# All four casts of one batch's first half on VectorE instead of two on GpSimd, in a retention and snake kernel on one Trainium2 core

## The chip, the cores and the metric

The kernel runs on 1 core of one Trainium2 chip. The core has several engines, each of which works through its own queue of instructions in order: TensorE (PE in the profile, with its weight loads as PEld), VectorE (DVE), ScalarE (ACT), GpSimd (POOL) and SyncE (SP, which here only issues DMAs). The engines wait for each other through semaphores. The metric is the device time of one execution in microseconds (us).

## The reference: a decayed attention without softmax, then a two-layer network

```python
# q, k, v: (8 batches, 8 heads, 576 positions, 64)
scores = scale * np.matmul(q, k.transpose(0, 1, 3, 2))
gamma = 1.0 - 2.0 ** (-5.0 - np.arange(H))
Dmat = np.where(rel >= 0, gamma[:, None, None] ** rel[None], 0.0)   # rel = i - j
ret = np.matmul(scores * Dmat, v)                # -> x: (4608 tokens, 512)
h = x @ w_in                                     # 512 -> 2048
s = np.sin(alpha * h)
g = h + s * s / (alpha + 1e-09)
out = g @ w_out                                  # 2048 -> 512
```

## The kernel before, in words

The attention is worked chunk by chunk. Because each weight gamma^(i-j) is a product of a factor of the query's position and one of the key's position, q and k are multiplied by these factors while they are cast from f32 to f16. Then plain matmuls and a mask of zeros and ones give the scores inside a chunk, and a running state (a sum of k times v, faded by a power of gamma from chunk to chunk) carries what lies before it.

Each batch has two halves of 256 positions (p = 0 and p = 1) and a rest of 64. For one half, q and k are each loaded as a 128x1024 f32 tile and cast in two quarters t = 0 and t = 1 (even and odd heads), 128x512 each. So one half has four casts, each one instruction in `cast_half` (line 215), a TENSOR_TENSOR of two tensors in SBUF (the loaded tile and the factors `cn`) into an f16 tile. The table's steps, one for each line, are these:

- `C b nm p t E` casts a quarter on engine E (V is VectorE, A ScalarE, G GpSimd).
- `TR b p nm` transposes k or q on TensorE (line 275), which needs both quarters of it; `TK` copies the transposed tile out of PSUM (lines 236 and 237). From batch 2's second half on, `CR b p` transposes by DMA instead, issued on SP's queue (line 232).
- `SP` computes scores on TensorE (line 376). `SM` masks them on VectorE (line 393), either straight from PSUM or, after `SO` has copied them to an f16 tile `scf` on ScalarE, from SBUF.
- `VA` (line 413) multiplies the masked scores with v, `ST` (line 439) adds the state's part, both on TensorE; `XT` copies the result out of PSUM as x (lines 236 and 237).
- `FA` (line 330) fades the running sum, `NS` (line 334, VectorE) adds the next chunk to it, `TS` (line 346) makes the f16 state from it.
- `G1` and `G2` are the two matrix products of the network (lines 535 and 574), with `SI` (sine, 544), `SQ` (square, 553 to 555) and `PR` (product, 560) between; `OS` copies a finished output block out of PSUM and issues its two stores on SP.
- `LK` loads q or k through SP; `LV` and `WO` load v and w_out through GpSimd's queue.

There are nine blocks of 512 tokens for the network: one for each batch's two halves, and one for all rests. The table `TABLE` writes out by hand the order of everything up to the end of block 1; the order of its lines is the order in each engine's queue. After it, a loop over blocks 2 to 8 interleaves the first product of a block with the second product of the block before, and puts the attention of the next batches between. The change is in the table, where block 0 is finished (`G2 0 ...`), batch 1's second half is worked (`VA 1 1`, `ST 1 1`), and batch 2's first half is prepared (lines 790 to 821):

```
TS 1 2 G        VA 1 1 1       SM 1 1 0       VA 1 1 0       ST 1 1
XT 1 1 A        OS 0 0 A       C 2 q 0 1 V    C 2 k 0 0 V    G2 0 3 3 hp
C 2 q 0 0 G     C 2 k 0 1 G    TR 2 0 k       TR 2 0 q       TK 2 0 k A
G1 1 0 hp       SI 1 0         FA 1 2 G       NS 1 3         OS 0 3 V
TS 1 3 G        C 2 k 1 1 G    C 2 k 1 0 G    C 2 q 1 1 G    C 2 q 1 0 G
CR 2 1          G1 1 1 hp      ...            TK 2 0 q V     SP 2 0 0
```

(It reads row by row.) So on VectorE the queue there is `SM 1 1 0`, the two casts marked V, `NS 1 3`, `OS 0 3`, `TK 2 0 q`; on GpSimd it is `TS 1 2`, the two casts marked G, `FA 1 2`, `TS 1 3`, and the four casts of batch 2's second half; on TensorE it is `VA 1 1 0`, `ST 1 1`, `G2 0 3 3`, `TR 2 0 k`, `TR 2 0 q`, `G1 1 0`, `G1 1 1`, `SP 2 0 0`. `SM 1 1 0` reads `scf`, that is, from SBUF.

Of the kernel before, what the change touches and what calls it, by code (L numbers as in the profile page):

```python
# [16 lines left out]
def kernel(  # L17
# [10 lines left out]
    nc = tc.nc  # L28
# [63 lines left out]
    alpha_t = const.tile([P, FC], F32, tag="alpha", bufs=1)  # L92
# [486 lines left out]
    def gemm2(n, u, bank):  # L579
        gemm2_pe(n, u, bank)  # L580
        c, part = divmod(u, 4)
        if part == 3:
            osb = work.tile([P, 512], F32, tag="osb", bufs=4, name="osb")
            nc.scalar.copy(osb, ops.pop((n, c)))  # L584
            for h in range(2):
                nc.sync.dma_start(rows_of(n, c, h), osb[halves(h)])
# [50 lines left out]
TS 0 1 V  # L637
NS 0 2
TS 0 2 G
AO  # L640
WI 2
TK 0 1 q AA
# [155 lines left out]
C 2 q 0 1 V  # L798
C 2 k 0 0 V
G2 0 3 3 hp  # L800
C 2 q 0 0 G
C 2 k 0 1 G
TR 2 0 k
TR 2 0 q
TK 2 0 k A
# [100 lines left out]
PR 1 13  # L906
PR 1 10
G1 1 14 hp
GN
G1 1 15 mm  # L910
VA 2 1 1
ST 2 1
# [10 lines left out]
LV 3 0  # L923
TS 2 3 G
CR 3 1
GN
"""

    HALVES = [(0, "k"), (0, "q"), (1, "k"), (1, "q")]
# [1 line left out]
    V, A_, G_ = nc.vector, nc.scalar, nc.gpsimd  # L931

    with tc.manual_schedule():
# [18 lines left out]
        al = {}  # L952

        def alpha():
            al["ps"] = psum.tile([P, FC], F32, tag="hp", bufs=3, name="al_ps")
            nc.tensor.matmul(al["ps"], alpha_r, eye, start=True, stop=True, is_transpose=True)

        def alpha_out():
            nc.scalar.copy(alpha_t, al["ps"])
            nc.vector.tensor_scalar_add(inva, alpha_t, 1e-9)  # L960
            nc.vector.reciprocal(inva, inva)

# [81 lines left out]

        second = [(n, u) for n in range(1, NBLK) for u in range(12 if n == NBLK - 1 else 16)]

        def next_second():
            n, u = second.pop(0)
            gemm2(n, u, "hp" if n == NBLK - 1 and u > 3 else "op")

        STEP = {
            "GN": next_second,
            "H1": pair_pe,
            "HS": pair_sine,
# [30 lines left out]
            "OS": put_out,  # L1085
            "KB": keep_busy,
            "AL": alpha,
            "AO": alpha_out,
        }

# [14 lines left out]
        for n in range(2, NBLK):  # L1105
# [39 lines left out]
            for u in range(16):  # L1145
                gemm1(n, u)
                for f in todo.get(u, []):
                    f()
                last = second[0][1] % 4 == 3
                if not last:  # L1150
                    square(n, u, A_)
                    product(n, u)
                next_second()
                if last:
                    square(n, u, A_)
                    product(n, u)
        while second:
            next_second()
# [42 lines left out]
```

## Time and profile before

| | us |
|---|---|
| median of 3 runs (lowest, highest) | 316.03 (314.01, 316.04) |
| the profiled execution, whole | 315.3 |
| its span, first to last instruction | 313.5 |

The granted TensorE clock of the profiled execution was 0.98 of full speed. By stages of the profiled execution (us from its start; busy time of each engine in us):

| stage | length | PE | DVE | ACT | POOL | GB/s |
|---|---|---|---|---|---|---|
| 0 to 50: weights, batch 0, most of block 0 | 50.00 | 42.75 | 33.40 | 30.61 | 31.22 | 214 |
| 50 to 53.5 | 3.50 | 3.50 | 2.86 | 0.00 | 2.66 | 292 |
| 53.5 to 57.1 | 3.60 | 1.46 | 3.60 | 1.17 | 2.98 | 243 |
| 57.1 to 59.7 | 2.60 | 2.60 | 2.16 | 1.50 | 1.06 | 102 |
| 59.7 to 85: block 1 with batch 2 | 25.30 | 23.50 | 20.03 | 22.10 | 22.29 | 169 |
| 85 to 226: the loop | 141.00 | 141.00 | 92.73 | 113.06 | 77.12 | 168 |
| 226 to 313.5: the loop's last blocks | 87.50 | 83.14 | 33.73 | 60.25 | 0.00 | 46 |

An engine that is busy for all of a stage need not be what sets its length: an instruction counts as busy from its start to its end, also when it is held up in between. A row is read by asking which engine waits for which; the chain of waits, which follows the last instruction back to what released it, gives that.

### The profile page before, as it was taken

What the parts mean: (1) busy time and instruction counts of PE and PEld (TensorE: products, weight loads), DVE (VectorE), ACT (ScalarE), POOL (GpSimd) and SP (SyncE); (2) the same over time, 40 slices, a digit from 0 to 9 for tenths busy, and PEclk for the clock granted to TensorE, in tenths of its full rate; (3) what the DMA queues carried; (4) which work ended last, traced back from release to release, by engine and by line L of the source; (5) the groups of instructions that cost most, each with busy time, mean ns of one, the idle gap of its engine ahead of it and who ended that gap; (6) DMA issues with size and microseconds to landing.
All of it is one profiled execution on the core that took longest, in us unless ns stands there. A gap on an engine that the chain in (4) does not pass through costs nothing.

```text
span 313.5 us, 7658 instructions
## 1 busy us (share of the span) xinstructions
PE 298.0 (95%) x3145; PEld 152.6 (49%) x3145; DVE 188.5 (60%) x265; ACT 228.7 (73%) x374; POOL 137.3 (44%) x160
## 2 busy tenths in 40 slices
PE   5799989799899999999999999999999999999994
PEld 4586444444444444444444444544444444444443
DVE  3688957798675365856866786645845343444401
ACT  1469862599688878887888788787887878888710
POOL 3778656769969965950593055024700000000000
PEclk9589999999999999999999999999999999999998
DMA  8999999796999899999999977689331111122133
GB/s 215 209 174 193 265 192 289 141 225 150 149 182 225 170 166 192 207 150 206 209 143 213 170 167 187 102 108 130 69 67 37 35 36 33 33 50 52 33 67 68
DMA packets 118018, 44.74 MB, mean 143 GB/s; under 512 B 84432, under 2 KB 113504, under 8 KB 117984
## 3 DMA queue, kind: packets, MB, share of 16 engines
q1 hardware_dynamic: 83792, 35.08, 58.5%
q0 software_dynamic: 33600, 8.92, 29.2%
q8 instruction: 24, 0.39, 0.6%
q10 hardware_dynamic: 592, 0.28, 0.4%
q14 instruction: 10, 0.08, 0.1%
HBM read 36.91 MB, written 9.44 MB: 148 GB/s over the span
## 4 chain that ended last, share of the span: by engine, by line
PE 80%; DVE 8%; DMA 4%; ACT 2%; POOL 2%; issue 1%; SPq 1%; DVEq 0%; POOLq 0%; ACTq 0%
PE ops L574 37%; PE hps L535 32%; DVE ret L393 4%; DMA qT<-q 2%; PE sc L376 2%; PE o L413 2%; DMA k<-in_k_dram 2%; DVE gT L560 2%; PE o L439 2%; PE tr L275 1%; PE kv L312 1%; PE ops L1163 1%; PE hps L1013 1%; DVE kvs L334 1%; DVE gT L1040 1%
## 5 line engine op out<-in xcount | busy, mean ns | idle before, releaser
L560 DVE SCALAR_TENSOR_TENSOR gT<-ss_t,inva,hps 128x512 f16<-128x512 f16 x136 | 100.4, 745 | 86.8 <-ACT ss_t L553 86.3
L574 PE MATMUL ops<-w_out,gT 128*128 128x512 f16 x560 | 140.8, 379 | 0.0
L535 PE MATMUL hps<-x,w_in 128*128 128x512 f16 x480 | 120.9, 379 | 1.3 <-DVE gT L560 1.1
L544 ACT ACTIVATE s_t<-hps,alpha_t 128x512 f16<-128x512 f32 x136 | 92.8, 685 | 33.0 <-PE hps L535 31.8
L535 PEld LDWEIGHTS <-w_in 128*128 128x128 f16 x544 | 52.8, 98 | 64.9 <-issue 1.9
L574 PEld LDWEIGHTS <-gT 128*128 128x128 f16 x560 | 52.7, 98 | 59.9 <-DVE gT L560 0.3
L553 ACT ACTIVATE ss_t<-s_t 128x512 f16<-128x512 f16 x127 | 79.9, 631 | 2.5
L346 POOL TENSOR_TENSOR s<-kvs,cn 128x512 f16<-128x512 f32 x28 | 30.5, 1091 | 56.2 <-ACT kvs L319 47.6
L584 ACT COPY osb<-ops 128x512 f32<-128x512 f32 x31 | 18.2, 586 | 13.2 <-PE ops L574 13.2
L126 POOL DMA_DIRECT2D v<-in_v_dram x32 | 22.0, 732 | 0.0
L236 ACT CAST x<-o 128x1024 f16<-128x1024 f32 (+1 forms) x17 | 14.9, 889 | 6.3 <-PE o L439 5.5
L393 DVE TENSOR_TENSOR ret<-sc,mask 128x1024 f16<-128x1024 f32 x12 | 14.4, 1214 | 5.7 <-PE sc L376 5.7
L215 DVE TENSOR_TENSOR q<-q,cn 128x512 f16<-128x512 f32 x17 | 14.4, 847 | 5.1 <-DMA q<-in_q_dram 4.9
L535 PE MATMUL hps<-x_rest,w_in 128*128 128x512 f16 x64 | 16.4, 379 | 0.0
L215 POOL TENSOR_TENSOR q<-q,cn 128x512 f16<-128x512 f32 x15 | 16.0, 1077 | 0.1
L393 DVE TENSOR_TENSOR ret<-sc,two 128x768 f16<-128x768 f32 x16 | 14.9, 950 | 0.0
L413 PE MATMUL o<-ret,v 64*64 64x128 f16 (+1 forms) x512 | 10.6, 218 | 3.4 <-DVE ret L393 2.5
L555 POOL TENSOR_TENSOR ss_t<-s_t 128x512 f16<-128x512 f16 x10 | 10.7, 1077 | 6.2 <-ACT s_t L544 4.9
L359 POOL TENSOR_TENSOR kvs<-s,kvs 128x256 f32<-128x256 f32 x15 | 12.5, 835 | 1.2
L376 PE MATMUL sc<-qT,kT 64*64 64x128 f16 (+1 forms) x512 | 11.2, 219 | 0.9 <-DMA qT<-q 0.6
L376 PEld LDWEIGHTS <-kT 64*64 64x64 f16 x512 | 8.2, 111 | 7.5 <-issue 5.1
L413 PEld LDWEIGHTS <-v 64*64 64x64 f16 x512 | 7.9, 110 | 7.5 <-issue 7.0
(69 smaller groups left out, 207.6 us busy)
## 6 DMA issues: line engine op xcount, KB each, us to landing
out_dram<-osb SPq DMA_DIRECT2D x70, 128.0 KB, 2.5
q<-in_q_dram SPq DMA_DIRECT2D x14, 512.0 KB, 6.8
k<-in_k_dram SPq DMA_DIRECT2D x32, 128.0 KB, 5.1
k<-in_k_dram SPq DMA_DIRECT2D x7, 512.0 KB, 6.8
q<-in_q_dram SPq DMA_DIRECT2D x8, 256.0 KB, 7.2
v<-in_v_dram POOLq DMA_DIRECT2D x8, 256.0 KB, 5.8
w_in<-in_moe_w_in_dram POOLq DMA_DIRECT2D x4, 512.0 KB, 6.9
w_out<-in_moe_w_out_dram POOLq DMA_DIRECT2D x4, 512.0 KB, 7.3
```

What stands on the lines that cost most here:

```text
L126: nc.gpsimd.dma_start(t_[halves(g), :, s], v[b, :, xs, :].rearrange("h i d -> i h d"))
L215: eng.tensor_tensor(half[b, nm, p][:, :, :, t, :], raw[b, nm, p].rearrange("p (a t) (r d) -> p a t r d", t=2, r=2)[:, :, t], (ct if nm == ...
L346: (eng or nc.gpsimd).tensor_tensor(d_, self.kvs[:, n].unsqueeze(2).to_broadcast([P, 4, 2, D]), g2.unsqueeze(3).to_broadcast([P, 4, 2, D]), ...
L376: nc.tensor.matmul(sc[halves(g), t, x : x + 128 - 64 * late], T[0][halves(t), 2 * a + r, halves(g)], T[1][halves(t), 2 * a : 2 * a + 2, 64 ...
L393: nc.vector.tensor_tensor(ret.rearrange("p t (z x) -> p (t z) x", z=2)[:, :, 0:n], sc.rearrange("p t (z x) -> p (t z) x", z=2)[:, :, 0:n], ...
L413: nc.tensor.matmul(o[g][halves(t), x0 : x0 + 128].rearrange("p (r i) -> p r i", r=2)[:, :, i0:], x, y, start=(t, g) not in begun, stop=las ...
L535: nc.tensor.matmul(hps, w_in16[:, a, fc * P : (fc + 1) * P], x_of[n][:, a], start=(a == 0), stop=(a == KT - 1),)
L544: nc.scalar.activation(s_t, hps, mybir.ActivationFunctionType.Sin, bias=0.0, scale=alpha_t[:, fc : fc + 1],)
L553: nc.scalar.activation(ss_t, s_t, mybir.ActivationFunctionType.Square)
L560: nc.vector.scalar_tensor_tensor(gT[n][:, fc, :], ss_t, inva[:, fc : fc + 1], hps, MULT, ADD)
L574: nc.tensor.matmul(ops[n, c], gT[n][:, fk, c * P : (c + 1) * P], w_out16[:, fk, :], start=(fk == 0), stop=(fk == FC - 1),)
L584: nc.scalar.copy(osb, ops.pop((n, c)))
```

## The change

Two letters in the table move the casts of q's quarter 0 and k's quarter 1 of batch 2's first half from GpSimd's queue to VectorE's. They stand in the table behind VectorE's other two casts and before `NS 1 3`. The step `AO` is split in two, `AC` (the copy of alpha on ScalarE) and `AO` (the two VectorE instructions), which stand one behind the other where `AO` stood; and `GN` takes a number that the function doesn't use.

```diff
 TS 0 2 G
+AC
 AO
...
 C 2 q 0 1 V
 C 2 k 0 0 V
 G2 0 3 3 hp
-C 2 q 0 0 G
-C 2 k 0 1 G
+C 2 q 0 0 V
+C 2 k 0 1 V
 TR 2 0 k
 TR 2 0 q
...
-GN
+GN 0
...
-GN
+GN 1
...
+        def alpha_copy():
+            nc.scalar.copy(alpha_t, al["ps"])
+
         def alpha_out():
-            nc.scalar.copy(alpha_t, al["ps"])
             nc.vector.tensor_scalar_add(inva, alpha_t, 1e-9)
             nc.vector.reciprocal(inva, inva)
...
-        def next_second():
+        def next_second(k=0):
             n, u = second.pop(0)
             gemm2(n, u, "hp" if n == NBLK - 1 and u > 3 else "op")
...
+            "AC": alpha_copy,
             "AO": alpha_out,
```

## The prediction, made before the changed kernel was run

> **What bounds the kernel now.** I read the busy time by engine first, then the chain of waits, then the timeline at the place of the change. The first two:
>
> ```profile
> PE 298.0 (95%) x3145; PEld 152.6 (49%) x3145; DVE 188.5 (60%) x265; ACT 228.7 (73%) x374; POOL 137.3 (44%) x160
> PE 80%; DVE 8%; DMA 4%; ACT 2%; POOL 2%; issue 1%; SPq 1%; DVEq 0%; POOLq 0%; ACTq 0%
> ```
>
> TensorE is busy for 95% of the span and carries 80% of the chain. From 85 to 226 us it has no idle time at all, so there VectorE's and GpSimd's loads decide nothing. The change can gain or lose only where TensorE waits around batch 2's first half. The chain of waits there (start, length, what):
>
> ```profile
> 52.39 1.20 DVE x L237 x2
> 53.59 3.45 DVE ret L393
> 57.04 0.04 issue
> 57.08 0.42 PE o L413 x16
> 57.50 0.55 PE o L439 x8
> 58.05 0.86 PE ops L574 x4
> 58.92 0.89 PE tr L275 x16
> 59.81 1.73 PE hps L535 x8
> ...
> 77.83 6.92 DMA qT<-q
> ```
>
> One VectorE instruction, the mask `SM 1 1 0` (L393), stands in it for 3.45 us; after it TensorE works without a gap through VA, ST, G2, the transposes and into block 1. The timeline there (start, length, engine, line, operation, tiles, in brackets the idle time before):
>
> ```profile
> 45.62 0.68 DVE L393 TENSOR_TENSOR ret<-scf,mask 128x1024 f16<-128x1024 f16 x1
> ...
> 52.85 1.05 POOL L346 TENSOR_TENSOR s<-kvs,cn 128x512 f16<-128x512 f32 x1
> ...
> 53.51 3.52 DVE L393 TENSOR_TENSOR ret<-scf,mask 128x1024 f16<-128x1024 f16 x1
> ...
> 53.86 1.05 POOL L215 TENSOR_TENSOR q<-q,cn 128x512 f16<-128x512 f32 x1
> ...
> 54.87 1.04 POOL L215 TENSOR_TENSOR k<-k,cn 128x512 f16<-128x512 f32 x1
> 55.87 0.60 POOL L330 TENSOR_TENSOR s<-kvs,cn 128x256 f32<-128x256 f32 x1
> 56.95 0.68 DVE L215 TENSOR_TENSOR q<-q,cn 128x512 f16<-128x512 f32 x1
> 57.08 0.42 PE L413 MATMUL o<-ret,v 64*64 64x128 f16 x16 [2.14 <-DVE ret L393]
> ```
>
> The same mask took 0.68 us at 45.62, while GpSimd did nothing, and 3.52 us here. It ends at 57.03, which is 0.56 us after GpSimd's unbroken row of four instructions ends (55.87 + 0.60 = 56.47). Elsewhere a VectorE instruction with two SBUF inputs behaves alike: a cast at 125.64 took 1.24 us instead of 0.68 and ended at 126.88, 0.55 us after GpSimd's L359 (125.60 + 0.73 = 126.33). A mask that reads its scores from PSUM took its usual 1.22 us at 97.53 beside GpSimd's L346. So I read the 3.52 us as 0.68 us of work and 2.84 us held up by GpSimd's row, in which the two casts that the change removes stand second and third.
>
> **The change part by part.** *Removed from GpSimd:* two casts, 1.05 + 1.04 us, 2.01 us by start to start (53.86 to 55.87). L346 stays, 52.85 to 53.90, and `FA 1 2` (L330, 0.60 us) now follows at about 53.86, since the sum that it reads was ready at 52.39. GpSimd's row ends at 54.46. If the mask again ends 0.56 us behind the row, it ends at 55.02, 2.01 us earlier. If it is let in at 53.90 it ends at 54.46; then FA waits (as an L358 at 124.47, 1.06 us instead of 0.61, did beside a cast) and delays the first cast.
>
> *Added to VectorE:* two casts. Three rows bear on their price: 0.68 us with GpSimd idle (56.95, and start to start 0.61, 56.95 to 57.56), 0.79 us at 124.26 and 1.24 to 1.47 us (125.64, 154.98) behind one GpSimd instruction. GpSimd is idle here until `NS 1 3`, which stands behind the casts, so I take 0.61 each. The first of four starts at 54.94 (0.08 before the mask ends, as before), and the last ends at 54.94 + 3 x 0.61 + 0.68 = 57.45. If the mask is let in early, the first cast waits for FA's end at about 54.92, ends 0.55 later at 55.47, and the last ends at 57.30: nearly the same.
>
> *Moved on TensorE:* VA starts at 55.07 instead of 57.08, ST and G2 follow, and G2 ends its turn near 56.75. Before, the transposes started at 58.75, straight behind G2, because the last cast was ready at 58.24. Now they need VectorE's fourth cast, at 57.45, and start at 57.5: TensorE waits 0.7 us anew. Of the 2.01 us, 58.75 - 57.50 = 1.25 us remain. Queued behind the transposes are both G1 and the scores of batch 2, which also need the two copies `TK`, free on both engines (ScalarE's x copy ends near 57.1, VectorE's `OS 0 3` near 58.4; the transposes end near 58.56).
>
> *Behind the added casts on VectorE:* `NS 1 3` ends at 57.8 instead of 58.57, so `TS 1 3` on GpSimd starts 0.8 us earlier, and its four casts of batch 2's second half end at 62.93 instead of 63.72. The next square there, at 64.10, waited 0.38 us for ScalarE; its sine comes at 62.83, so GpSimd is 0.1 us behind, with the product that needs it not yet due. SP's queue holds the two DMA transposes of `CR 2 1` and then batch 3's loads. Its first transpose was held by the output stores until 62.62 and the second until 64.13; now the casts hold the second, to about 62.96, so loads are issued 1.15 us earlier. They land at 71.58 for q, first half (66.08 + 5.5), used at 72.20: slack 0.62; and at 76.73 for its second half (68.23 + 8.5), used at 77.37: slack 0.64. With uses 1.25 and loads 1.15 earlier, 0.5 us of slack stays. No wait on a load is new for the moved casts: GpSimd read both tiles by 53.86 and 54.87 without waiting.
>
> *Afterwards* TensorE waits 0.59 us at 84.88 for the DMA transpose `CR 3 0`, issued from 76.49 behind a GpSimd row that starts with a square at 70.00, itself waiting 0.72 us for ScalarE. So this wait moves with the rest, and the stage from 59.7 on moves as a whole. `AC`, `AO` and `GN` keep every queue's order: nothing.
>
> The sum: -2.01 (hold-up) + 0.76 (transposes now waiting for casts) = -1.25 us. The profiled execution (span 313.5, 1.8 around it, 315.3) becomes 314.05; by the median of 316.03, which lies 0.7 above it, 314.8. I take 314.4, between.
>
> The Trainium skill, "SBUF — State Buffer", section "Who interferes with whom", says that a VectorE instruction with two SBUF inputs and a GpSimd instruction that reads SBUF exclude each other, for the whole instruction of the one that came first. On the exclusion the trace agrees (3.52 against 0.68 us). On its extent it doesn't: by the rule the mask should have been let in at 53.90, after one instruction, and it waited for four. By that rule the casts held nothing, and the change gives the slower rival below.
>
> **The rivals.** *The hold-up stays (slower).* For: three times VectorE was let in between two GpSimd instructions: a cast at 124.26 (0.79 us, ending 0.55 after L346), one at 154.98, and a square at 75.15 (0.41 us) amid a GpSimd row from 70.00 to 76.46. So the row of four may not be what held the mask. Against: the end 0.56 us behind exactly that row. Then the mask still ends at 57.03, four casts end at 56.95 + 3 x 0.61 + 0.68 = 59.46, and the transposes start at 59.5 instead of 58.75: +0.75 us, 316.05 by the profiled execution, 316.8 by the median. It decides from the point where the mask ends later than 56.3, since the fourth cast then comes after 58.70.
>
> *A second hold-up eats the gain.* The square at 75.15 asked for its inputs within 0.1 us of a boundary between two GpSimd instructions (75.21). GpSimd is forecast 0.1 us off the rest; if the square misses the boundary, it ends behind the row at 76.46 + 0.27 instead of 75.56, 1.17 us late (0.27 as at 21.49, where the square ended at 22.40 behind a GpSimd end at 22.11). Net about -0.1: 315.2 to 315.9.
>
> *More is gained.* TensorE is idle for 25.30 - 23.50 = 1.8 us between 59.7 and 85, partly behind collisions of this kind (GpSimd squares of 1.24 us at 70.00, casts of 1.25 at 75.21). If some fall away as engines shift, up to about 0.75 us more: -2.0, 313.3.
>
> **How the numbers follow.** Forecast 0.60; hold-up stays 0.17; second hold-up 0.13; more gained 0.10. The low end is 313.3 less 0.5, since the runs of before reach 1.3 below the profiled execution; the high end is 316.8, the slower rival on the median. Range 312.8 to 316.8. One per cent, about what a measurement of this kernel can tell from no change, is 3.2 us. None of the cases passes that by its own size: the gain would need all of TensorE's idle time in the stage, the loss several new hold-ups in a row. Both signs get something for a run of such effects and for the 0.6% by which runs of the same kernel differ: faster 0.13, within 0.78, slower 0.09.
>
> **What would show it.** Right: the mask of 3.52 us falls to 0.9 to 1.5; four VectorE casts in a row at 0.61 start to start; TensorE's wait of 2.14 us before VA nearly gone, and a new one of 0.6 to 0.7 us before the transposes, which start at 57.3 to 57.5; the wait at 84.88 near 83.7. Wrong: a mask still over 2.5 us; casts over 1 us; a square after 70 us that waits behind GpSimd; loads of batch 3 awaited on GpSimd.

## The result, and the profile after

| | before | changed |
|---|---|---|
| median, us (lowest, highest; 22 executions each, taken together) | 316.39 (314.01, 318.10) | 314.49 (313.45, 317.23) |
| ratio, with its 95% interval | | 0.9953 [0.9933, 0.9974] |
| the profiled execution / its span, us | 315.3 / 313.5 | 316.3 / 314.5 |

The ratios here, and the counts in the last section, leave out the few executions that took over 1.5% longer than the fastest of their kernel.

The changed kernel is faster by 0.5%, about 1.5 us by the ratio: the interval lies clear of 1, and the difference is under one per cent. Its profiled execution is one of the longer of the 22, and longer than the profiled one of before, so the spans must not be compared as they stand. Distances from one event show what the change did. I count from the start of the mask `SM 1 1 0`: before at 53.51 us, after at 53.92 us.

The chain of waits after, at the place of the change (start, length, what):

```profile
52.80 1.20 DVE x L237 x2
54.00 1.44 DVE ret L393
55.44 0.60 DVE q L215
56.04 0.60 DVE k L215
56.65 0.60 DVE q L215
57.25 0.60 DVE k L215
57.85 0.34 DVE kvs L334
58.19 0.04 issue
58.23 1.05 PE tr L275 x16
59.29 1.73 PE hps L535 x8
```

The timeline of the same place:

```profile
53.26 1.06 POOL L346 TENSOR_TENSOR s<-kvs,cn 128x512 f16<-128x512 f32 x1
...
53.92 1.53 DVE L393 TENSOR_TENSOR ret<-scf,mask 128x1024 f16<-128x1024 f16 x1
...
54.27 0.62 POOL L330 TENSOR_TENSOR s<-kvs,cn 128x256 f32<-128x256 f32 x1
...
57.77 0.41 DVE L334 TENSOR_TENSOR kvs<-s,kv 128x256 f32<-128x256 f32 x1
...
58.23 0.61 PE L275 MATMUL tr<-ident,k 128*128 128x128 f16 x8 [0.90 <-DVE kvs L334]
```

The mask falls from 3.52 to 1.53 us and ends 0.56 us behind GpSimd's row, which is now two instructions long (54.27 + 0.62 = 54.89; 53.92 + 1.53 = 55.45). TensorE's wait of 2.14 us before `VA` is gone. In its place VectorE stands in the chain with four casts and with `NS 1 3` (L334): the transposes, which have to wait 0.90 us, are released by `NS 1 3`, not by the last cast: they start 0.05 us after `NS 1 3` ends (57.77 + 0.41 = 58.18), and 0.38 us after the cast (57.85). The reason is in the code:

```python
kv2 = psum.tile([P, 2, 512], F32, tag="mm", bufs=2, name="kv")
...
self.tr_of[p] = psum.tile([P, 2, 1024], F16, tag="mm", bufs=2, name="tr"), []
```

The transposes' tile in PSUM takes one of the two `mm` buffers, and that buffer still holds the sum `kv`, which `NS 1 3` is the last to read. In the trace of before, `NS 1 3` and the first transpose stood here:

```profile
58.16 0.41 DVE L334 TENSOR_TENSOR kvs<-s,kv 128x256 f32<-128x256 f32 x1
...
58.75 0.61 PE L275 MATMUL tr<-ident,k 128*128 128x128 f16 x8
```

First transpose: 58.75 - 53.51 = 5.24 us behind the mask's start before, 58.23 - 53.92 = 4.31 after. The first mask of batch 3, about 31 us behind, tells how much of this is kept (before, then after):

```profile
85.35 2.35 DVE L393 TENSOR_TENSOR ret<-sc,mask 128x1024 f16<-128x1024 f32 x2 [0.62 <-PE sc L376]
```

```profile
84.57 2.36 DVE L393 TENSOR_TENSOR ret<-sc,mask 128x1024 f16<-128x1024 f32 x2 [0.68 <-PE sc L376]
```

Where the trace then loses more than this, near 121 us (before, then after; timeline, the number in brackets is the idle time in front and what ended it):

```profile
119.81 1.29 DVE L215 TENSOR_TENSOR k<-k,ct 128x512 f16<-128x512 f32 x2 [2.17 <-DMA k<-in_k_dram]
```

```profile
120.27 2.42 DVE L215 TENSOR_TENSOR k<-k,ct 128x512 f16<-128x512 f32 x2 [3.41 <-DMA k<-in_k_dram]
...
123.41 1.02 PE L535 MATMUL hps<-x,w_in 128*128 128x512 f16 x4 [1.74 <-DVE gT L560]
```

VectorE waits 3.4 instead of 2.2 us for a load of batch 5, its two casts then take 2.42 instead of 1.29 us beside GpSimd's instructions, and the products queued behind them make TensorE wait 1.74 us. The account of this execution closes: it comes to the mask 0.41 us later; it is 1.19 us shorter from there to the first mask of batch 3 (84.57 - 53.92 = 30.65 against 85.35 - 53.51 = 31.84); and it waits 1.74 at 121. The sum, +0.96, is the 1.0 by which the spans differ. So in this execution the wait at 121 takes back more than was won before it.

### The profile page after: what moved, and what is told of

Read it like the earlier page. It is cut to its first block, busy times and chain, and to the rows that moved or that the text cites. A ratio compares the mean times of both kernels' runs of the same rounds, so it can differ in the third digit from the quotient of the medians.

```text
span 314.5 us, 7656 instructions
## 1 busy us (share of the span) xinstructions
PE 298.1 (95%) x3145; PEld 152.8 (49%) x3145; DVE 188.5 (60%) x267; ACT 228.5 (73%) x374; POOL 135.4 (43%) x158
## 3 DMA queue, kind: packets, MB, share of 16 engines
q1 hardware_dynamic: 83792, 35.08, 57.3%
## 4 chain that ended last, share of the span: by engine, by line
PE 67%; POOL 8%; DVE 8%; DMA 7%; SPq 5%; issue 2%; ACT 1%; DVEq 0%; POOLq 0%
PE ops L574 31%; PE hps L535 26%; DMA k<-in_k_dram 7%; SPq L147 3%; POOL k L215 3%; DVE ret L393 3%; POOL q L215 2%; PE o L413 2%; PE sc L376 2%; DVE gT L560 1%; PE tr L275 1%; PE o L439 1%; PE ops L1167 1%; POOL ss_t L555 1%; POOL s L346 1%
## 5 line engine op out<-in xcount | busy, mean ns | idle before, releaser
L346 POOL TENSOR_TENSOR s<-kvs,cn 128x512 f16<-128x512 f32 x28 | 30.3, 1084 | 58.2 <-ACT kvs L319 48.5
L215 DVE TENSOR_TENSOR q<-q,cn 128x512 f16<-128x512 f32 x18 | 15.3, 850 | 4.9 <-DMA q<-in_q_dram 4.9
L215 POOL TENSOR_TENSOR q<-q,cn 128x512 f16<-128x512 f32 x14 | 14.6, 1058 | 0.1
L215 DVE TENSOR_TENSOR k<-k,ct 128x512 f16<-128x512 f32 x12 | 9.6, 817 | 3.4 <-DMA k<-in_k_dram 3.4
```

The source lines that it names most:

```text
L215: eng.tensor_tensor(half[b, nm, p][:, :, :, t, :], raw[b, nm, p].rearrange("p (a t) (r d) -> p a t r d", t=2, r=2)[:, :, t], (ct if nm == ...
L346: (eng or nc.gpsimd).tensor_tensor(d_, self.kvs[:, n].unsqueeze(2).to_broadcast([P, 4, 2, D]), g2.unsqueeze(3).to_broadcast([P, 4, 2, D]), ...
```

## The experiments

Each kernel is the one before or the changed one with a small edit, and ratios are to the kernel before on the same chip. "First transpose" and "first mask of batch 3" are distances from the mask's start.

**e1, the changed kernel again.**

> The changed kernel once more, for a second trace. All distances are from the start of the mask SM 1 1 0. Theory (GpSimd's unbroken row holds the mask, and the transposes of batch 2 wait for NS 1 3, which the added casts push back): mask 1.5 us; first transpose at 4.3 (before 5.24); first mask of batch 3 at 30.7 (before 31.84); ratio to the kernel before 0.993 to 0.998. The wait of 1.7 us that TensorE had near 121 us in the first trace, for a late load of k, comes and goes from execution to execution: it need not be there. Rival (that wait belongs to the change): it is there again, and the whole gain of 1 us in the early stage is given back in this execution too.

Measured: 314.66 us, ratio 0.9944 [0.9915, 0.9973]. Mask 1.52, first transpose 57.24 - 52.93 = 4.31, first mask of batch 3 at 30.09. TensorE's wait near 121 us is there again, 1.66 us, so here the rival was right: nearly all that was won is given back. Still the span is 312.9: 0.58 earlier at the mask, 1.75 shorter up to batch 3, 1.66 lost, together -0.67 against -0.6. What is left is about the 0.58, and that can't be put down to the change: over the 14 traces the mask starts between 52.32 us (e10) and 54.27 us (e5), in kernels with and without the change alike.

**e2, one cast moved.**

```diff
-C 2 q 0 0 V
+C 2 q 0 0 G
 C 2 k 0 1 V
```

> Only k's quarter 1 moves to VectorE; q's quarter 0 stays on GpSimd. Theory (the row holds the mask until it ends): the row is TS, one cast, FA, and the mask takes 0.39 + 1.01 + 0.60 + 0.56 = about 2.55 us; three casts on VectorE, NS 1 3 ends at 4.67, first transpose at about 4.7 from the mask's start (before 5.24, both moved 4.31). Time about half way, 0.5 us under before. Rival one (the mask is let in behind the first GpSimd instruction, something else held it before): the mask is 3.5 or 0.95 us, not 2.5. Rival two (it is all or nothing): 1.5 us.

Measured: 315.70 us, ratio 0.9969 [0.9934, 1.0004]. The timeline of e2:

```profile
53.61 2.52 DVE L393 TENSOR_TENSOR ret<-scf,mask 128x1024 f16<-128x1024 f16 x1
53.96 1.05 POOL L215 TENSOR_TENSOR q<-q,cn 128x512 f16<-128x512 f32 x1
54.97 0.60 POOL L330 TENSOR_TENSOR s<-kvs,cn 128x256 f32<-128x256 f32 x1
```

The mask lies half way, 0.56 us behind the end of a row that is one cast shorter than before, and the first transpose comes at 58.32 - 53.61 = 4.71. Both rivals fall: each cast in the row costs the mask its length. The time lies between the two kernels, but its interval reaches 1.

**e3, the row put back, the casts left on VectorE.**

```diff
+DU 2 q 0 0
+DU 2 k 0 1
...
+        def dummy(b, nm, p, t):
+            d_ = work.tile([P, 4, 2, D], F16, tag="dum", bufs=2, name="dum")
+            nc.gpsimd.tensor_tensor(d_, ...)
```

> As the changed kernel, all four casts on VectorE, but GpSimd also makes two casts of the same size into a scratch tile, where its two casts stood: extra work that nothing reads. This separates the row on GpSimd from the place of the casts. Theory: the mask takes 3.5 us again, then come four casts and NS 1 3: first transpose at 3.44 + 4 x 0.60 + 0.41 + 0.05 = 6.3 from the mask's start, 1.1 later than before and 2.0 later than with the change; time 1.0 us over before, ratio near 1.003. Rival (the mask's 3.5 us had another cause, which the move took away): mask 1.5 us, first transpose 4.3, time as with the change.

Measured: 316.71 us, ratio 1.0011 [0.9977, 1.0045]. The timeline of e3, then its busy times for each us (stretch and length; then PE, PEld, DVE, ACT and POOL busy; then the granted clock of TensorE, the DMA share and GB/s):

```profile
53.08 3.52 DVE L393 TENSOR_TENSOR ret<-scf,mask 128x1024 f16<-128x1024 f16 x1
...
53.43 1.05 POOL L1058 TENSOR_TENSOR dum<-q,cn 128x512 f16<-128x512 f32 x1
...
54.43 1.04 POOL L1058 TENSOR_TENSOR dum<-k,cn 128x512 f16<-128x512 f32 x1
```

```profile
57.00:58.00 1.00, 1.00 (x18) 0.75 (x12) 1.00 (x3) 0.34 (x1) 0.00 (x0) 1.00 0.66 146
58.00:59.00 1.00, 0.81 (x3) 0.00 (x0) 1.00 (x3) 1.00 (x2) 0.00 (x0) 0.51 0.00 0
59.00:60.00 1.00, 0.61 (x7) 0.71 (x8) 0.94 (x3) 0.16 (x1) 0.58 (x1) 0.50 0.00 0
60.00:61.00 1.00, 1.00 (x12) 1.00 (x11) 0.00 (x0) 0.00 (x0) 1.00 (x2) 0.50 0.75 160
61.00:62.00 1.00, 1.00 (x7) 0.49 (x5) 0.69 (x1) 0.71 (x1) 1.00 (x2) 0.78 0.94 201
```

The mask takes 3.52 us again, with all casts on VectorE. So the 2.0 us belong to GpSimd's row, not to the place of the casts. The first transpose is at 59.39 - 53.08 = 6.31, as forecast: this is what two more casts cost when nothing is won for them. What I had not forecast is in the second fence: TensorE's clock is granted at half for 3.4 us, from about 58.0 to 61.4. With it the first mask of batch 3 comes at 33.64, 1.80 behind before and not 1.07. The time can't be told from before (e1, without the extra row, lies below it, and the two intervals don't meet).

**e4, another order.**

```diff
 OS 0 0 A
+FA 1 2 G
+NS 1 3
-C 2 q 0 1 V
 C 2 k 0 0 V
+C 2 k 0 1 V
 G2 0 3 3 hp
+C 2 q 0 1 V
 C 2 q 0 0 V
-C 2 k 0 1 V
+SEH 2 q 0
 TR 2 0 k
+G1 1 0 hp
 TR 2 0 q
 TK 2 0 k A
-G1 1 0 hp
 SI 1 0
-FA 1 2 G
-NS 1 3
...
+            "SEH": lambda b, nm, p: seen(G_, half[b, nm, p][:, 0, 0, 0, 0:1]),
```

> As the changed kernel, but VectorE does NS 1 3 before the four casts, then k's two, then q's two; TensorE puts G1 1 0 between the transposes of k and q; and GpSimd waits for the last cast (a copy of one element) before TS 1 3, so that its next row doesn't start beside them. Theory (the transposes waited for NS 1 3 behind four casts): mask 1.5, last cast ends at 4.3, the transposes of k start straight behind G2 at about 3.3 instead of 4.3, those of q at about 4.5 behind G1 1 0, and everything behind comes 0.9 us earlier than with the change: first mask of batch 3 near 29.8; time 0.9 us under the changed kernel, ratio to before near 0.992. Rival (the copies of the transposed tiles, or GpSimd's later start, are next): first mask of batch 3 unchanged at 30.7.

Measured: 313.51 us, ratio 0.9919 [0.9890, 0.9948]. The timeline of e4:

```profile
54.42 0.41 DVE L334 TENSOR_TENSOR kvs<-s,kv 128x256 f32<-128x256 f32 x1
...
54.75 1.28 DVE L215 TENSOR_TENSOR k<-k,cn 128x512 f16<-128x512 f32 x2
...
55.96 1.28 DVE L215 TENSOR_TENSOR q<-q,cn 128x512 f16<-128x512 f32 x2
...
56.22 0.61 PE L275 MATMUL tr<-ident,k 128*128 128x128 f16 x8
```

The same instructions as in the changed kernel, plus a copy of one element: with `NS 1 3` first, the transposes of k start at 56.22 - 52.97 = 3.25, straight behind `G2`, and batch 3's first mask comes at 29.90 (30.65 and 30.09 with the change). e4 changes the place of `NS 1 3`, the order of the casts and the place of `G1 1 0` at once, so it shows only that these together take the transposes' wait away. That `NS 1 3` held them rests on the traces with the old order: in after, e1, e2, e3 and e6 alike the first transpose starts 0.05 us behind the end of `NS 1 3`. This trace has the wait near 121 us too (1.73 us).

**e5, the same order without the guard.** As e4, without the line `SEH 2 q 0`.

> As e4, but GpSimd doesn't wait for the last cast: TS 1 3 and its four casts of the second half (five instructions without a gap, 5.1 us) run beside VectorE's four casts. This tells how far a hold-up reaches. All distances from the start of the mask SM 1 1 0. Theory (GpSimd keeps VectorE out until its unbroken row ends): VectorE's first cast ends at 2.5, GpSimd's row from there to about 7.6, the second cast ends at 8.1, first transpose at about 8.2 (e4: 3.25); time about 4 us over e4, ratio to before near 1.004. Rival (each instruction gives the port up at its end): the second cast ends near 4.0, the third near 5.6, the fourth near 7.1; first transpose at 4.1; ratio near 0.996 to 1.000. If VectorE's casts run on as a row of their own: as e4, ratio 0.992.

Measured: 316.79 us, ratio 1.0020 [0.9993, 1.0048]. The timeline of e5, VectorE's part and GpSimd's:

```profile
56.05 2.13 DVE L215 TENSOR_TENSOR k<-k,cn 128x512 f16<-128x512 f32 x2
58.10 2.98 DVE L215 TENSOR_TENSOR q<-q,cn 128x512 f16<-128x512 f32 x2
```

```profile
56.21 1.42 POOL L346 TENSOR_TENSOR s<-kvs,cn 128x512 f16<-128x512 f32 x1 [0.97 <-DVE kvs L334]
57.59 2.94 POOL L215 TENSOR_TENSOR k<-k,cn 128x512 f16<-128x512 f32 x2
```

Here my theory fell on its reach. The second cast ends at 58.18, 0.55 us behind the end of GpSimd's one instruction (56.21 + 1.42 = 57.63), not behind a row of five, and the two engines then take turns: two casts of 1.28 us become 2.13 and 2.98, two of GpSimd's of 2.05 become 2.94. The second cast ends 3.91 behind the mask's start (rival: 4.0; theory: 8.1). The Trainium skill, "SBUF — State Buffer", section "Who interferes with whom", says that the one that comes second is blocked for the whole instruction of the other, and taking turns fits that. On these casts the trace agrees with it; on the mask, which waited for rows of two, three and four, it doesn't. The early stage loses nearly all that e4 won (first mask of batch 3 at 31.81), and the time is between the 1.004 of the theory and the 0.996 to 1.000 of the rival.

**e6, the mask freed without moving a cast.** A copy of one element of the mask's result is put into GpSimd's queue of the kernel before, so that its casts wait for the mask.

```diff
 SM 1 1 0
+SER 1 1 0
...
+            "SER": lambda b, p, y: seen(G_, of(b).ret[p, y][:, 0, 0:1]),
```

> The kernel before, with both casts left on GpSimd, but GpSimd first waits for the mask SM 1 1 0 (it copies one element of it), so that no row stands before the mask. This takes the hold-up of the mask away without moving a cast. Theory (the transposes wait for the four casts, FA 1 2 and NS 1 3, wherever the hold-up falls): the mask takes 0.95 us, but then the casts of both engines meet, NS 1 3 ends near 5.1, and the first transpose is at 5.1 to 5.3 from the mask's start, as before (5.24); ratio 0.997 to 1.001. Rival (the mask's hold-up alone is what the change won): first transpose near 4.3 or less; ratio near 0.994.

Measured: 315.54 us, ratio 0.9977 [0.9948, 1.0006]. The timeline of e6:

```profile
53.13 0.96 DVE L393 TENSOR_TENSOR ret<-scf,mask 128x1024 f16<-128x1024 f16 x1
...
57.81 0.42 DVE L334 TENSOR_TENSOR kvs<-s,kv 128x256 f32<-128x256 f32 x1 [2.52 <-POOL s L330]
...
58.28 0.61 PE L275 MATMUL tr<-ident,k 128*128 128x128 f16 x8 [2.08 <-DVE kvs L334]
```

The mask takes 0.96 us, and almost nothing is won: the first transpose is at 58.28 - 53.13 = 5.15, since `NS 1 3` now waits 2.52 us for `FA 1 2`, and GpSimd has the casts to do first. Freeing the mask is not enough here: with the casts still on GpSimd, which does one in about 1.04 us against VectorE's 0.60, the transposes are held at their other end. (Whether it would do to put `FA 1 2` ahead of the casts in this kernel was not tried.)

**e7, batch 5's casts later; e8, with e4's order.** In the changed kernel (e7) and in e4 (e8):

```diff
-                for i, u in enumerate(CASTS[n > 2]):
+                for i, u in enumerate((3, 3, 4, 4, 6, 8, 9, 10) if n == 3 else CASTS[n > 2]):
```

> The changed kernel, with the four casts of batch 5's first half two units (about 3.5 us) later in the loop: k's two in unit 3 instead of 1, q's in unit 4 instead of 3 and 4. In both traces of the changed kernel TensorE waits 1.7 us near 121 us, since VectorE waits 3.4 us there for k, and the second cast is then held up by GpSimd (the pair takes 2.3 to 2.4 us instead of 1.29), with the products queued behind. Theory (this gives back a part of what the change wins): the wait is gone; ratio to before near 0.990, 1.5 us under the changed kernel. Rival (the wait is there in some executions only, or the casts meet GpSimd's instructions again where they now stand): ratio 0.994 to 0.996.

> e4 (the other order, GpSimd waiting) together with e7 (batch 5's casts later). Theory: both gains add up, since one lies before 62 us and the other near 121 us: ratio to before near 0.987. Rival (e4's trace has the same wait of 1.7 us near 121 us but not most of its executions): as e4, 0.992.

Measured: e7 313.34 us (6 executions, 313.12 to 314.57), ratio 0.9914 [0.9885, 0.9943]; e8 313.06 us (6 executions, 312.77 to 314.13), ratio 0.9903 [0.9875, 0.9931]. In both traces the wait near 121 us is gone, and e7's early stage is that of the changed kernel (first mask of batch 3 at 84.03 - 53.22 = 30.81). The account closes again: e8 is at the mask 0.31 earlier than before, first mask of batch 3 at 83.24 - 53.20 = 30.04, 1.80 shorter; the sum of -2.11 against 311.4 - 313.5 = -2.1. e8 has the lowest median of all kernels run, but the 0.987 of its theory lies just outside its interval, and e7's ratio and the 0.992 of the rival inside. In the traces both gains stand: the wait is gone, and batch 3 is reached 0.77 us sooner than in e7. In the times it isn't shown that they add up.

**e9, the kernel before again; e10, it with e7's edit alone.**

> The kernel before once more, for a second trace: it tells whether TensorE's wait of 1.6 to 1.8 us near 121 us (in the traces of the changed kernel twice, e4, e5, e6; not in the first trace of before, e2, e3) belongs to the change or comes and goes in every kernel. Theory (it comes and goes): either answer can be seen in one trace, so the number to look at is e10; here mask 3.5 us, first transpose at 5.24 from the mask's start; ratio 1.000. Rival (an earlier early stage brings the wait): not there, VectorE's wait for k about 2 us.

> The kernel before with e7's one edit, batch 5's casts two units later. Theory (the wait near 121 us comes in part of the executions of every kernel, the one before too, and makes the spread of its times): ratio 0.994 to 0.997 and a spread of about 1.5 us instead of 4. Rival (the wait belongs to the change and costs it a part of its gain): ratio 1.000, spread as before.

Measured: e9 315.14 us, ratio 0.9991 [0.9960, 1.0022]; mask 3.52, first transpose 5.24, no wait near 121 us, VectorE's wait for k 1.72 us. e10 316.94 us, ratio 1.0032 [0.9994, 1.0070], spread 313.61 to 318.46. So e10's edit wins nothing in the kernel before, and the theory that the wait near 121 us makes its spread fell. Nor is it simply the mark of an earlier start: e5 and e6 have it (1.8 and 1.6 us) and reach batch 3 no earlier than before. The load itself takes longer: from the first of its four issues to the first cast that reads it pass 10.0 to 10.2 us in after, e1, e4, e5 and e6, and 8.8 to 9.2 us in before, e9, e2, e3 and e11. e12 (next) lies between, with 9.8 us and a wait of 1.11 us; it and e6 are the kernel before with one small edit, so the wait is not the change's alone. What makes that load take 1 us more is open.

**e11 and e12, why the mask is held for a whole row.** Two edits in the kernel before: the mask's scores as f32 (e11), or the mask as two instructions (e12).

```diff
+            if (self.b, p, y) == (1, 1, 0):
+                scf = work.tile([P, 2, 512], F32, tag="scf32", bufs=1, name="scf32")
```

```diff
+            parts = 2 if (self.b, p, y) == (1, 1, 0) else 1
+            for i in range(parts):
+                tz = slice(4 // parts * i, 4 // parts * (i + 1))
```

> The kernel before, with the scores of the mask SM 1 1 0 copied to an f32 tile instead of f16, so that this one mask reads f32 (own work about 1.2 us, as the masks from PSUM). In e5 a cast from f32 was let in after one GpSimd instruction; the f16 mask was held over two, three and four. Theory (what decides is the kind of VectorE instruction: 16-bit operands wait for the end of the row): the mask is let in behind TS, at 0.39 from its start, and takes about 1.5 us. Rival (what decides is the row on GpSimd): held until the row's end at 2.96, it takes 4.0 to 4.1 us.

> The kernel before, with the mask SM 1 1 0 as two f16 instructions of 512 elements a partition instead of one of 1024. Theory (16-bit operands wait for the end of the row, whatever the length): the first half takes 3.2 us, the second 0.4, first transpose as before at 5.2 to 5.4. Rival (the length decides): the first half is let in behind TS and takes 0.7 us, the second waits for one GpSimd instruction, about 1.3.

Measured: e11 317.47 us, ratio 1.0059 [1.0024, 1.0095]; e12 316.05 us, ratio 1.0002 [0.9964, 1.0041]. The masks in the two timelines (in these kernels they stand in line 396):

```profile
53.98 4.05 DVE L396 TENSOR_TENSOR ret<-scf,mask 128x1024 f16<-128x1024 f32 x1
```

```profile
53.20 3.25 DVE L396 TENSOR_TENSOR ret<-scf,mask 128x512 f16<-128x512 f16 x1
```

In e11 the theory fell: a mask whose scores are f32 is held to the row's end as well, and the kernel is slower than before by 0.6%. In e12 the length is ruled out: half a mask waits as long. e12's forecast for the first transpose, 5.2 to 5.4, missed: it came at 59.86 - 53.20 = 6.66, because the granted clock fell to 0.50 from about 57.0 us and `G2`'s four matmuls took 1.91 instead of 1.03 us. So neither the type of the scores nor the length of the VectorE instruction explains the difference from e5's casts (the mask itself and the result were f16 in all runs). One difference is left in the traces: in e5 GpSimd's first instruction had itself been made to wait (1.42 instead of 1.05 us), while the row in front of the mask ran unhindered. But two casts in the loop of before (124.26 and 154.98) were let in behind an unhindered L346, so this doesn't settle it, and it was not tried by itself. When a row is given up in between stays open.

## Why the prediction was right, point by point

- *The hold-up:* forecast -2.01 us at the mask's end. Measured 3.52 to 1.53, -1.99. That GpSimd's row causes it is shown by e2 and e3.
- *Two casts at 0.61 on VectorE:* four stand at 55.44, 56.04, 56.65 and 57.25, 0.60 apart.
- *The transposes:* forecast 1.25 us earlier, measured 0.93. The mis-sized term is "+0.76 (transposes now waiting for casts)"; it is 1.06 us, because what they wait for is `NS 1 3`, 0.3 us behind the last cast. So the new wait is 0.90 us and not 0.6 to 0.7, and on the scale of the trace before the transposes start at 53.51 + 4.31 = 57.82 and not at 57.3 to 57.5. The prediction went by the inputs of the transposes and not by who still reads the buffer of their output. Its own rows could have told: before, `NS 1 3` ended at 58.16 + 0.41 = 58.57, only 0.18 us ahead of the first transpose.
- *The stage from 59.7 on moves as a whole:* not quite. Up to batch 3 the gain grew to 1.19 us in the first trace, where TensorE's wait of 0.64 us at 71.04 fell to 0.31, and to 1.75 in e1, where the wait for `CR 3 0` (0.59 us at 84.88) is gone too; in e7 it is 1.03. That is a part of the rival *More is gained*. The square at 75.15, at which I expected the second hold-up, took 0.53 instead of 0.41 us, so that hold-up stayed away.
- *The rivals:* with the casts on VectorE, the full hold-up came back only where the row was put back (e3). Something like the second hold-up did come, but 45 us later than I had placed it: two casts beside GpSimd's instructions near 121 us, behind a late load, 1.7 us in both traces of the changed kernel. The loop, in which "VectorE's and GpSimd's loads decide nothing", is not free of them.
- *The number:* 314.4 against 314.49, inside 312.8 to 316.8, and within 1%. That it is so close is luck. The median gain is 1.9 us (1.5 by the ratio), the gain at the transposes 0.93; and in both traces of the changed kernel the wait near 121 us, which the forecast doesn't have, takes back what was won up to batch 3 (1.74 us against 1.19, 1.66 against 1.75). The forecast has no term for the clock either. The last section has what probably fills the difference.

## What to carry to other kernels

When a VectorE instruction with two inputs in SBUF shows several times its usual length (here 3.52 instead of 0.68 us), look at what GpSimd runs beside it before working on the instruction itself. When a step is said to be free, look for the last reader of the buffer that it writes, not only for its inputs. And compare two traces by distances from one event, stage by stage: here the trace of the better kernel was the longer one.

## What the hardware showed that I had not expected

A TensorE gap of about 2 us can cost nearly as much again. In four of the seven traces with such a gap here the granted clock fell to 0.50 for 3.4 us (e3; e6 from about 59.1, e11 from 58.4, e12 from 57.0), after waits of 1.88 to 2.67 us; in the three others (before, e9, e10, 2.14 us each) it stayed at 1.00, and none of the seven traces whose longest wait between 54 and 62 us is 1.42 us or less had such a stretch there. The price can be read from e12, which does the work of the kernel before with the mask in two halves: its first mask of batch 3 comes at 86.75 - 53.20 = 33.55, against 31.84, 31.88 and 31.98 in before, e9 and e10, 1.6 to 1.7 us later. The Trainium skill, "TensorE: Matmul & The Clock Gate", section "What's actually happening", has a free-running window of about 3.4 us, of which an idle one halves the clock. The length agrees; that gaps of 1.9 to 2.7 us, shorter than such a window, are enough, and only in some executions, is what these traces add, and it fits a window that doesn't start with the kernel.

The mean clock that is listed for every execution sorts the 14 traces here: 0.978, 0.978, 0.992 and 0.993 with that stretch; 0.980 to 0.984 and 0.997 to 1.000 without. (The two levels of each sort come from a longer stretch at half clock in the first 20 us, which some traces have and others not: from about 8 to 17 us in before, none in e10.) Sorted by the same bounds (below 0.9795, or 0.987 to 0.9955), 39 of 96 executions of the kernel before in the three later comparisons, e9 among them, belong to the first sort, with a median of 316.86 us, and 57 to the second, with 314.99. Of the changed kernel 5 of 34 belong to the first (314.49) and 29 to the second (314.61). On the one chip on which e1 and the kernel before ran in the same comparison it is 16 of 29 for before (317.3 against 315.44 us) and none of 12 for the changed kernel (314.66). So the change seems to win 0.4 us in an ordinary execution over all chips, 0.8 us on that one, and to take away a loss of 1.9 us that four in ten of the executions of before had, since it closes the 2.14 us gap of TensorE. This is worked out from mean clocks, which are a rough mark: the changed kernel's five of the first sort are no longer than its others, and no trace of the kernel before itself shows the stretch. No experiment shows it.
